# Gate and value products of two token blocks in seven half-size products a unit

## The chip, the cores and the metric

The kernel runs on one core of a Trainium2 chip. The metric is the device time of one execution in microseconds, the median over several executions.

## The reference, cut to what matters

Cosine-weighted linear attention over 8 batches of 8 heads, 576 positions and 64 features each, gives `x`, 4608 tokens of 512 features. Then a gated feed-forward block follows:

```python
g = x @ w_gate                                   # 512 -> 1536
gelu = 0.5 * g * (1.0 + erf(g * inv_sqrt2))
val = x @ w_val                                  # 512 -> 1536
return (gelu * val @ w_out).astype(np.float32)   # 1536 -> 512
```

## The kernel before

**Blocks and units.** The 4608 tokens are nine blocks of 512 (`NB` = 9, numbered 0 to 8). The work is written in an order by hand: the pools run under a manual schedule, so each engine executes its instructions in the order of the program. The token activations lie transposed in SBUF, `xT[n]`, 128 partitions by 4 feature chunks (`CT`) by 512 tokens. A gate-and-value unit (`gv_unit`, lines 392 to 412) makes one of the twelve slices (`JT` = 12) of 128 hidden features of a block: four matmuls over the chunks into one PSUM bank with `wg_sb`, four into the next with `wv_sb` (line 401, 512 columns each), a Gelu on ScalarE from PSUM to `gel` (409), and a product on VectorE of `gel` with the value bank, written as bfloat16 to `hT[n]` (410). Units take the bank pairs 0-1 and 2-3 in turn.

**Output products.** The output projection of block n-1 runs between the units of block n. It is already done with seven products in place of eight, per group `p` of 128 tokens in each half of the block (two groups a block). `h_sum` (484 to 494) makes the operand sums S1 to S4 of `hT` on VectorE, 128x768 in bfloat16; `wo_sum` made those of `w_out` once (T1 to T4). `product` (503 to 543) issues six matmuls of 256 columns (510) into the halves of bank 4 or into bank 5, copies products 1, 6 and 7 to SBUF on ScalarE (`u`, 530) while TensorE goes on accumulating in the same place, and adds on VectorE into `o_sb` (524). Finished tiles are stored from SP's queue (`flush`, 423).

**The loop.** The main loop (743 to 823) runs blocks 1 to 8 and, inside, the twelve units. After each unit come one or two products of the block before (772; two in units 0 and 6, one in the others, fourteen a block) and the sums that the table `SUMS` names (774). Until block 6 it also holds the attention work of the next batch: `kv_unit`, `nm_unit`, `prep`, transposes by DMA (`turn_q`, `turn_x`). In blocks 7 and 8 there is no attention work left; for block 8, `h_sum` makes its own S3 at units 8 and 9, and at unit 11 the first four of six slices of S1, S2 and S4 (752 to 757). The tail (826 to 838) does the fourteen products of block 8 with the last two slices of the sums ahead of them.

**Tiles that the change takes over.** The input tiles `qf`, `kf`, `vf` (two buffers each), the mapped inputs `qp` and `kp`, and `qT` are not used for attention any more in the last blocks.

Of the kernel before, what the change touches and what calls it, by code (L numbers as in the profile page):

```python
# [9 lines left out]
FP32 = mybir.dt.float32  # L10
BF16 = mybir.dt.bfloat16
AF = mybir.ActivationFunctionType
ALU = mybir.AluOpType
# [3 lines left out]
def kernel(  # L17
# [13 lines left out]
    nc = tc.nc  # L31
# [3 lines left out]
    C = H * D  # L35
# [29 lines left out]
    def bank(i):  # L65
        return ps[:, i]
# [356 lines left out]
    def flush(engs=(nc.sync, nc.sync)):  # L423
        for i, o_sb in stores:
            store(engs, i, o_sb)
        stores.clear()
# [45 lines left out]
    def place(n, p, name, cols, dtype):  # L472

        if n < NB - 1:
            return sums.tile([128, cols], dtype, name=name)
        was = "q" if name[0] == "u" else "kv"[p]
        if was not in rest:
            n_el = 8 * CH if was == "q" else 4 * JH * 128
            rest[was] = [inp.tile([128, n_el], dtype, name=was + "f"), 0]
        t, at = rest[was]  # L480
        rest[was][1] += cols
        return t[:, at:at + cols]

    def h_sum(n, p, name, j0=0, j1=JH):
        a = hs.setdefault((n, p), h_parts(n, p))
        if name not in a:
            a[name] = place(n, p, name, JH * 128, BF16).rearrange("q (j t) -> q j t", j=JH)
        x, y, op = {
            "S1": ("A21", "A22", ALU.add),
            "S2": ("S1", "A11", ALU.subtract),  # L490
            "S3": ("A11", "A21", ALU.subtract),
            "S4": ("A12", "S2", ALU.subtract),
        }[name]
        nc.vector.tensor_tensor(a[name][:, j0:j1], a[x][:, j0:j1], a[y][:, j0:j1], op=op)  # L494

    PROD = {
        1: ("A11", "B11"), 2: ("A12", "B21"), 3: ("S4", "B22"), 4: ("A22", "T4"),
# [5 lines left out]
    def product(n, p, i, u, m, v):  # L503


        a, b = PROD[i]
        key = n, p
        at = {1: u, 6: u, 7: u, 5: m, 3: m, 2: v, 4: v}[i]
        for j in range(JH):
            nc.tensor.matmul(  # L510
                at,
                lhsT=hs.setdefault(key, h_parts(n, p))[a][:, j],
                rhs=ts[b][:, j],
                start=(j == 0 and i in (1, 2, 4, 5)),
                stop=(j == JH - 1),
                skip_group_check=i in (3, 6, 7),
            )
        if key not in got:
            got[key] = [outp.tile([128, C], FP32, name="o_sb") for _ in range(2)]
        lo, hi = got[key]  # L520
        last = n == NB - 1

        def add(o, k, x, op=ALU.add):
            nc.vector.tensor_tensor(o, got[key, k], x, op=op)  # L524

        if i in (1, 6, 7) or last and i == 5:
            if last and i == 7:
                add(hi[:, RIGHT], 5, u)
            got[key, i] = place(n, p, f"u{i}", CH, FP32)
            nc.scalar.copy(got[key, i], at)  # L530
        if i == (2 if last else 1):
            add(lo[:, LEFT], 1, v)
        if i == 7 and not last:
            add(hi[:, RIGHT], 7, m)
        if i == 4:
            add(hi[:, LEFT], 7, v, ALU.subtract)
        if i == 3:
            add(lo[:, RIGHT], 6, m)
        if i in (3, 4):
            flush()  # L540
            stores.append((4 * n + 2 + p, hi) if i == 4 else (4 * n + p, lo))
            if last:
                flush((nc.sync, nc.scalar if p == 1 and i == 4 else nc.sync))


    HALF = BLK // 2
# [171 lines left out]
    for n in range(4, B - 2):  # L718
# [6 lines left out]
    SUMS = {  # L725
        2: {0: "1", 1: "2", 2: "34", 3: "56", 6: "78"},
        3: {0: "1", 1: "23", 2: "4", 3: "56", 4: "7", 6: "8"},
        8: {0: "1", 1: "2", 2: "3", 3: "4", 6: "5", 7: "6", 8: "7", 9: "8"},
    }
    for n in range(4, 8):  # L730
        SUMS[n] = {0: "1", 1: "23", 2: "4", 3: "5", 4: "6", 5: "7", 6: "8"}


    q3 = {
# [5 lines left out]
        (2, 1): ((8,), ()),  # L740
    }
    turn[0] = 1
    for n in range(1, NB):
        b = n + 1

        t_kv, t_nm, t_turn = {1: (7, 9, 12), 2: (6, 7, 11), 3: (2, 5, 9)}.get(n, (1, 2, 8))
        for jt in range(JT):
# [1 line left out]
                nm_unit(2, jt - t_nm, (6, 4, 6)[jt - t_nm])  # L749
                turn_x(2, jt - t_nm)  # L750
            heads = (0, 2, 4, 2)[n] if n < 4 else 0
            if n == NB - 1 and jt in (8, 9):
                h_sum(n, jt - 8, "S3")
            if n == NB - 1 and jt == JT - 1:
                for p in range(2):
                    for name in ("S1", "S2", "S4"):
                        h_sum(n, p, name, 0, JH - 2)
            if jt >= heads:
                gv_unit(n, jt)
            else:  # L760
# [60 lines left out]
                        turn_x(c, i)  # L821
            if n == 1 and 4 <= jt < 8:
                wo_sum(f"T{jt - 3}")


    for what in (
        ["S1", "S2", "S4", (0, 1), (1, 1), (0, 2, 0 + 2 * (turn[0] % 2)), (0, 5), (0, 6)]
        + ["T1", "T2", "T4", (1, 2, 1 + 2 * (turn[0] % 2)), (0, 3), (0, 7), (1, 5), (0, 4, 0)]
        + [(1, 6), (1, 3), (1, 7), (1, 4, 1)]
    ):  # L830
        if isinstance(what, str):
            h_sum(NB - 1, "ST".index(what[0]), "S" + what[1], JH - 2, JH)
        else:
            p, i = what[:2]
            to = (what[2:] or (0,))[0]
            product(
                NB - 1, p, i, ps[:, 4 + 2 * p, 0:CH], ps[:, 5 + 2 * p, 0:CH], ps[:, to, 0:CH]
            )


# [28 lines left out]
```

## Time and profile before

| | |
|---|---|
| median of 3 runs | 318.5 us (318.33 to 318.73) |
| the profiled execution | 319.06 us |
| its span, first to last instruction | 316.9 us |
| TensorE clock granted, mean | 0.996 |
| blocks 7 and 8, from the first matmul of block 7 to the last of the tail | 243.3 to 312.1 us |
| PE busy in 243.3 to 273.2 | 29.74 of 29.90 us |

A page or a view comes from one execution under the hardware profiler. PE is TensorE's matmul row, PEld its weight loads, which overlap it, DVE is VectorE, ACT ScalarE, POOL GpSimd, SP the queue that issues most DMAs. A matmul's recorded length includes its way through the pipeline, so matmuls in a row start closer together than their lengths say; their pace is read from start to start. Some matmul records are missing. "Idle before" is the time for which an engine had nothing that could start, with the instruction that released it. The chain is followed back from the last instruction, each step to what it waited for.

### The profile page before, as it was taken

To read this page: it belongs to the slowest core of one execution; us is meant where nothing else is said; L and a number is where in the kernel's file an instruction comes from. 1 tells how busy PE (TensorE), PEld (TensorE's weight loads), DVE (VectorE), ACT (ScalarE), POOL (GpSimd) and SP (SyncE) were. 2 spreads that over 40 slices of the span, in tenths; PEclk is the share of its full clock that TensorE was granted. 3 is DMA by queue.
4 is the path that set the end of the run, shared out by engine and by line. 5 is a ranking of instruction groups with operands and counts; after the bars stand their busy time and mean duration, and the time that the engine had idled before them with its cause. 6 is when DMAs were issued, how large, how long until landed. Compare 5 with 4: busy or idle time off the path is not lost.

```text
span 316.9 us, 7015 instructions
## 1 busy us (share of the span) xinstructions
PE 306.9 (97%) x2692; PEld 191.8 (61%) x2727; DVE 224.7 (71%) x542; ACT 159.4 (50%) x356; POOL 26.0 (8%) x43
## 2 busy tenths in 40 slices
PE   8899999999999999999999999999999999999994
PEld 2574455655866676666665566556666565656583
DVE  5854695699897996798687859695944554454782
ACT  7864675956474754466328632773232323232321
POOL 6674430000000000000000000000000000000000
PEclk9999999999999999999999999999999999999998
DMA  7999999871798946995993699175342020202025
GB/s 268 245 178 245 312 320 402 259 149 38 241 202 300 304 99 179 370 163 133 319 272 88 152 369 232 34 150 109 76 86 50 17 68 0 66 2 67 2 67 132
DMA packets 68945, 53.61 MB, mean 169 GB/s; under 512 B 45360, under 2 KB 54064, under 8 KB 68912
## 3 DMA queue, kind: packets, MB, share of 16 engines
q1 hardware_dynamic: 59184, 41.23, 49.7%
q0 software_dynamic: 9648, 11.80, 16.1%
q8 instruction: 21, 0.34, 0.4%
q10 hardware_dynamic: 80, 0.13, 0.1%
q14 instruction: 12, 0.10, 0.1%
HBM read 37.75 MB, written 9.44 MB: 149 GB/s over the span
## 4 chain that ended last, share of the span: by engine, by line
PE 86%; DMA 8%; issue 1%; DVE 1%; POOL 1%; SPq 0%; ACT 0%; DVEq 0%; POOLq 0%
PE ps L401 56%; PE ps L510 23%; DMA qf<-in_q_dram 4%; PE ps L283 3%; PE ps L242 2%; DMA vf<-in_v_dram 2%; DMA wv_sb<-in_moe_w_val_dram 2%; PE ps L373 1%; PE ps L431 1%; PE ps L358 0%; DVE x_sb L296 0%; SPq L81 0%; POOL wg_sb L95 0%; DVE o_sb L524 0%; POOL gate L560 0%
## 5 line engine op out<-in xcount | busy, mean ns | idle before, releaser
L410 DVE TENSOR_TENSOR hT<-gel,ps 128x512 bf16<-128x512 f32 (+1 forms) x114 | 73.5, 648 | 55.8 <-PE ps L401 50.3
L401 PE MATMUL ps<-xT,wv_sb 128*128 128x512 bf16 (+1 forms) x450 | 109.4, 364 | 0.3
L401 PE MATMUL ps<-xT,wg_sb 128*128 128x512 bf16 (+1 forms) x431 | 107.4, 363 | 1.5 <-issue 0.3
L409 ACT ACTIVATE gel<-ps 128x512 f32<-128x512 f32 (+1 forms) x114 | 64.4, 566 | 78.6 <-PE ps L401 72.3
L401 PEld LDWEIGHTS <-wv_sb 128*128 128x128 bf16 x456 | 44.6, 98 | 47.1
L401 PEld LDWEIGHTS <-wg_sb 128*128 128x128 bf16 x456 | 41.7, 98 | 28.2 <-issue 0.3
L510 PEld LDWEIGHTS <-S 128*128 128x128 bf16 x336 | 32.9, 98 | 14.9 <-DVE S L494 0.9
L530 ACT COPY u<-ps 128x256 f32<-128x256 f32 x42 | 15.6, 372 | 43.4 <-PE ps L510 43.4
L510 PE MATMUL ps<-T,S 128*128 128x256 bf16 x252 | 34.4, 273 | 0.0
L161 ACT ACTIVATE qp<-qf,sin_t 128x256 bf16<-128x256 f32 x72 | 32.0, 501 | 3.7 <-DMA qf<-in_q_dram 3.7
L524 DVE TENSOR_TENSOR o_sb<-u,ps 128x256 f32<-128x256 f32 x56 | 23.4, 418 | 14.4 <-ACT u L530 14.4
L510 PEld LDWEIGHTS <-hT 128*128 128x128 bf16 x288 | 28.2, 98 | 8.8
L161 ACT ACTIVATE kp<-kf,sin_t 128x256 bf16<-128x256 f32 (+1 forms) x73 | 30.0, 480 | 1.0 <-DMA kf<-in_k_dram 1.0
L296 DVE TENSOR_TENSOR x_sb<-ps,rec 128x512 bf16<-128x512 f32 x38 | 26.3, 692 | 2.0 <-DMA xT<-x_sb 0.5
L163 DVE TENSOR_SCALAR qp<-qf,cos_t 128x256 bf16<-128x256 f32 x71 | 22.0, 357 | 3.3 <-DMA qf<-in_q_dram 3.3
L510 PE MATMUL ps<-wo_sb,hT 128*128 128x256 bf16 x192 | 23.6, 273 | 0.0
L163 DVE TENSOR_SCALAR kp<-kf,cos_t 128x256 bf16<-128x256 f32 x63 | 18.2, 349 | 0.0
L283 PEld LDWEIGHTS <-qT 128*128 128x128 bf16 x304 | 14.6, 98 | 2.8 <-ACT qT L588 0.3
L283 PE MATMUL ps<-kv_sb,qT 128*128 128x65 bf16 x304 | 16.0, 194 | 0.0
L494 DVE TENSOR_TENSOR S<-hT 128x768 bf16<-128x768 bf16 x28 | 15.4, 552 | 0.0
L510 PE MATMUL ps<-T,hT 128*128 128x256 bf16 x96 | 13.1, 273 | 0.2
L180 DVE CAST vx<-vf 128x1152 bf16<-128x1152 f32 (+1 forms) x15 | 11.9, 802 | 1.0 <-DMA vf<-in_v_dram 1.0
(84 smaller groups left out, 204.8 us busy)
## 6 DMA issues: line engine op xcount, KB each, us to landing
out_dram<-o_sb SPq DMA_DIRECT2D x71, 128.0 KB, 2.5
kf<-in_k_dram SPq DMA_DIRECT2D x12, 576.0 KB, 7.2
vf<-in_v_dram SPq DMA_DIRECT2D x12, 576.0 KB, 8.7
qf<-in_q_dram SPq DMA_DIRECT2D x10, 576.0 KB, 5.2
qf<-in_q_dram POOLq DMA_DIRECT2D x4, 576.0 KB, 12.4
kf<-in_k_dram POOLq DMA_DIRECT2D x4, 576.0 KB, 12.5
vf<-in_v_dram POOLq DMA_DIRECT2D x4, 576.0 KB, 12.6
wg_sb<-in_moe_w_gate_dram POOLq DMA_DIRECT2D x6, 256.0 KB, 6.8
```

The source lines that it names most:

```text
L161: nc.scalar.activation(o, i, AF.Relu, scale=tab[:, j:j + 1])
L163: (eng or nc.vector).tensor_scalar(o, i, 0.0, tab[:, j:j + 1], op0=ALU.max, op1=ALU.mult)
L180: copy(vx_tiles[b % 2][:, m0:m1, j0:j1, 0:D], staged["v", b][:, m0:m1, j0 * D:j1 * D].rearrange("p m (j d) -> p m j d", d=D),)
L283: nc.tensor.matmul(bank(b0 + h // 4)[:, (h % 4) * (D + 1):(h % 4 + 1) * (D + 1)], lhsT=q_cols(b, t, h), rhs=kv_sb[b][:, h // 2, h % 2, :], ...
L296: nc.vector.tensor_tensor(x, nm[:, :, :, 0:D], rec[:, :, :, None].to_broadcast([128, 2, 4, D]), op=ALU.mult,)
L401: nc.tensor.matmul(bank(b0 + g)[:, 0:w], lhsT=wt[:, ct, js], rhs=xt[:, ct, c0:c0 + w], start=(ct == 0), stop=(ct == CT - 1),)
L409: nc.scalar.activation(gel[:, 0:w], bank(b0)[:, 0:w], AF.Gelu)
L410: nc.vector.tensor_mul(hT[n][:, jt, c0:c0 + w], gel[:, 0:w], bank(b0 + 1)[:, 0:w])
L494: nc.vector.tensor_tensor(a[name][:, j0:j1], a[x][:, j0:j1], a[y][:, j0:j1], op=op)
L510: nc.tensor.matmul(at, lhsT=hs.setdefault(key, h_parts(n, p))[a][:, j], rhs=ts[b][:, j], start=(j == 0 and i in (1, 2, 4, 5)), stop=(j == ...
L524: nc.vector.tensor_tensor(o, got[key, k], x, op=op)
L530: nc.scalar.copy(got[key, i], at)
```

## The change

**Units of blocks 7 and 8.** The loop runs blocks 1 to 6 (`FAST` = 7). For blocks 7 and 8 a new `fast_unit` treats gate and value weights together as a 2 by 2 matrix of blocks: rows are gate and value, columns the lower and upper two of the four feature chunks; the right-hand side is `xT[n]`, split by the same chunks and by halves of 256 tokens. Seven products replace eight. Each is two matmuls of 256 columns. The partial results are combined in place: product 1 goes to one of the banks 2, 6, 7, is copied by ScalarE into half of bank 0, where product 2 is added on top; product 6 is added onto 1, copied to SBUF (`U6`), then product 7 and later 4 are added in the same place. Product 5 goes to bank 3 or 1, is copied to SBUF (`M5`), and product 3 is added onto it. VectorE adds `U6` and that bank into SBUF (`G2`, the gate of the second half of the tokens), and `M5` and product 7 back into the bank in PSUM (the value of the second half). Two Gelus and two products of 256 columns replace one of each of 512.

**Two units at a time.** In step t, products 1 and 5 of unit t come first, then product 7 of unit t-1, the output products (`o_step`) of one unit, products 6, 2 and 3 of unit t, and product 4 of unit t-1. So 25 steps serve 24 units, and `o_step` lags by one step.

**Sums.** `w_sum` makes S1 to S4 of the two weights (128x2x1536, in three pieces each, twelve instructions of 128x2x512) on VectorE in block 6, at units 0, 1 and 7 to 11. `x_sum` makes T1 to T4 of a block's `xT` (128x512): those of block 7 at units 8 to 11 of block 6, those of block 8 after steps 2, 4, 6 and 8 of block 7. The operand sums `h_sum` of blocks 6 and 7, and most of those of block 8, move from VectorE to GpSimd; block 8's second group keeps three on VectorE, in the tail, whole.

**Tail.** One product of block 8 moves into the last step; the thirteen others have a new order, with product 3 of the second group last. Product 5's contribution comes from its SBUF copy, so one VectorE addition there has two SBUF inputs. The stores of both last tiles use SP's and ScalarE's queue.

In the instruction order of TensorE, 144 matmuls and 144 weight loads come on top: 24 units by 14 - 8.

```diff
--- before.py
+++ after.py
@@ -473,15 +473,15 @@
 
         if n < NB - 1:
             return sums.tile([128, cols], dtype, name=name)
-        was = "q" if name[0] == "u" else "kv"[p]
+        was = "kp" if name[0] == "u" else ("kf", "vf")[p]
         if was not in rest:
-            n_el = 8 * CH if was == "q" else 4 * JH * 128
-            rest[was] = [inp.tile([128, n_el], dtype, name=was + "f"), 0]
+            pool, n_el = (attn, 8 * CH) if was == "kp" else (inp, 4 * JH * 128)
+            rest[was] = [pool.tile([128, n_el], dtype, name=was), 0]
         t, at = rest[was]
         rest[was][1] += cols
         return t[:, at:at + cols]
 
-    def h_sum(n, p, name, j0=0, j1=JH):
+    def h_sum(n, p, name, j0=0, j1=JH, eng=nc.vector):
         a = hs.setdefault((n, p), h_parts(n, p))
         if name not in a:
             a[name] = place(n, p, name, JH * 128, BF16).rearrange("q (j t) -> q j t", j=JH)
@@ -491,7 +491,7 @@
             "S3": ("A11", "A21", ALU.subtract),
             "S4": ("A12", "S2", ALU.subtract),
         }[name]
-        nc.vector.tensor_tensor(a[name][:, j0:j1], a[x][:, j0:j1], a[y][:, j0:j1], op=op)
+        eng.tensor_tensor(a[name][:, j0:j1], a[x][:, j0:j1], a[y][:, j0:j1], op=op)
 
     PROD = {
         1: ("A11", "B11"), 2: ("A12", "B21"), 3: ("S4", "B22"), 4: ("A22", "T4"),
@@ -524,14 +524,12 @@
             nc.vector.tensor_tensor(o, got[key, k], x, op=op)
 
         if i in (1, 6, 7) or last and i == 5:
-            if last and i == 7:
-                add(hi[:, RIGHT], 5, u)
             got[key, i] = place(n, p, f"u{i}", CH, FP32)
             nc.scalar.copy(got[key, i], at)
         if i == (2 if last else 1):
             add(lo[:, LEFT], 1, v)
-        if i == 7 and not last:
-            add(hi[:, RIGHT], 7, m)
+        if i == 7:
+            add(hi[:, RIGHT], 7, got[key, 5] if last else m)
         if i == 4:
             add(hi[:, LEFT], 7, v, ALU.subtract)
         if i == 3:
@@ -540,7 +538,119 @@
             flush()
             stores.append((4 * n + 2 + p, hi) if i == 4 else (4 * n + p, lo))
             if last:
-                flush((nc.sync, nc.scalar if p == 1 and i == 4 else nc.sync))
+                flush((nc.sync, nc.scalar if p == 1 else nc.sync))
+
+    FAST = NB - 2
+    CP = CT // 2
+    wa, xb, temps = {}, {}, {}
+
+    def w_sum(name, j0, j1):
+        if not wa:
+            wa["A11"], wa["A12"] = wg_sb[:, 0:CP], wg_sb[:, CP:CT]
+            wa["A21"], wa["A22"] = wv_sb[:, 0:CP], wv_sb[:, CP:CT]
+        if name not in wa:
+            was = {"S1": "qf", "S2": "qf", "S3": "kf", "S4": "vf"}[name]
+            wa[name] = inp.tile([128, CP, J], BF16, name=was)
+        x, y, op = {
+            "S1": ("A21", "A22", ALU.add),
+            "S2": ("S1", "A11", ALU.subtract),
+            "S3": ("A11", "A21", ALU.subtract),
+            "S4": ("A12", "S2", ALU.subtract),
+        }[name]
+        nc.vector.tensor_tensor(
+            wa[name][:, :, j0:j1], wa[x][:, :, j0:j1], wa[y][:, :, j0:j1], op=op
+        )
+
+    def x_sum(n, i):
+        if n not in xb:
+            xt = xT[n]
+            xb[n] = {
+                "B11": xt[:, 0:CP, 0:256], "B12": xt[:, 0:CP, 256:512],
+                "B21": xt[:, CP:CT, 0:256], "B22": xt[:, CP:CT, 256:512],
+            }
+        if "x" not in temps:
+            temps["x"] = attn.tile([128, 2, 4, CP, 256], BF16, name="qp")
+        b = xb[n]
+        x, y = (("B12", "B11"), ("B22", "T1"), ("B22", "B12"), ("B21", "T2"))[i]
+        b[f"T{i + 1}"] = temps["x"][:, n - FAST, i]
+        nc.vector.tensor_tensor(b[f"T{i + 1}"], b[x], b[y], op=ALU.subtract)
+
+    GV = {
+        1: ("A11", "B11"), 2: ("A12", "B21"), 3: ("S4", "B22"), 4: ("A22", "T4"),
+        5: ("S1", "T1"), 6: ("S2", "T2"), 7: ("S3", "T3"),
+    }
+    gels = {}
+
+    def fast_unit(t, between):
+
+        def at(i, t):
+            if i == 2:
+                return ps[:, 0, 256 * (t % 2):256 * (t % 2) + 256]
+            return bank((3, 1)[t % 2] if i in (3, 5) else (2, 6, 7)[t % 3])[:, 0:256]
+
+        def mm(i, t):
+            n, jt = FAST + t // JT, t % JT
+            a, b = GV[i]
+            for ct in range(CP):
+                nc.tensor.matmul(
+                    at(i, t),
+                    lhsT=wa[a][:, ct, jt * 128:(jt + 1) * 128],
+                    rhs=xb[n][b][:, ct],
+                    start=(ct == 0 and i in (1, 5)),
+                    stop=(ct == CP - 1),
+                    skip_group_check=i not in (1, 5),
+                )
+
+        def tmp(i, t):
+            if "t" not in temps:
+                temps["t"] = attn.tile([128, 6, 256], FP32, name="qT")
+            return temps["t"][:, 2 * i + t % 2]
+
+        def h(t, half):
+            n, jt = FAST + t // JT, t % JT
+            if n not in hT:
+                hT[n] = ffn.tile([128, JT, BLK], BF16, name="hT")
+            return hT[n][:, jt, 256 * half:256 * half + 256]
+
+        def gelu(t, half, src):
+            if t not in gels:
+                gels[t] = ffn.tile([128, BLK], FP32, name="gel")
+            nc.scalar.activation(gels[t][:, 256 * half:256 * half + 256], src, AF.Gelu)
+
+        new, old = t < 2 * JT, t > 0
+        M5, U6, G2 = range(3)
+        if new:
+            mm(1, t)
+            nc.scalar.copy(at(2, t), at(1, t))
+            mm(5, t)
+            nc.scalar.copy(tmp(M5, t), at(5, t))
+        if old:
+            mm(7, t - 1)
+            gelu(t - 1, 1, tmp(G2, t - 1))
+            nc.vector.tensor_tensor(at(3, t - 1), tmp(M5, t - 1), at(7, t - 1), op=ALU.add)
+            nc.vector.tensor_tensor(
+                h(t - 1, 1), gels[t - 1][:, 256:512], at(3, t - 1), op=ALU.mult
+            )
+        between()
+        if new:
+            mm(6, t)
+            nc.scalar.copy(tmp(U6, t), at(6, t))
+            mm(2, t)
+            gelu(t, 0, at(2, t))
+            mm(3, t)
+            nc.vector.tensor_tensor(tmp(G2, t), tmp(U6, t), at(3, t), op=ALU.add)
+        if old:
+            mm(4, t - 1)
+            nc.vector.tensor_tensor(
+                h(t - 1, 0), gels[t - 1][:, 0:256], at(4, t - 1), op=ALU.mult
+            )
 
     HALF = BLK // 2
@@ -725,10 +835,12 @@
     SUMS = {
         2: {0: "1", 1: "2", 2: "34", 3: "56", 6: "78"},
         3: {0: "1", 1: "23", 2: "4", 3: "56", 4: "7", 6: "8"},
-        8: {0: "1", 1: "2", 2: "3", 3: "4", 6: "5", 7: "6", 8: "7", 9: "8"},
+        8: {i: str(i + 1) for i in range(8)},
     }
     for n in range(4, 8):
         SUMS[n] = {0: "1", 1: "23", 2: "4", 3: "5", 4: "6", 5: "7", 6: "8"}
+
+    W_SUMS = {0: (0,), 1: (1,), 7: (2, 3, 4), 8: (5, 6), 9: (7, 8), 10: (9, 10), 11: (11,)}
 
     q3 = {
@@ -740,7 +852,7 @@
         (2, 1): ((8,), ()),
     }
     turn[0] = 1
-    for n in range(1, NB):
+    for n in range(1, FAST):
         b = n + 1
 
         t_kv, t_nm, t_turn = {1: (7, 9, 12), 2: (6, 7, 11), 3: (2, 5, 9)}.get(n, (1, 2, 8))
@@ -749,12 +861,6 @@
                 nm_unit(2, jt - t_nm, (6, 4, 6)[jt - t_nm])
                 turn_x(2, jt - t_nm)
             heads = (0, 2, 4, 2)[n] if n < 4 else 0
-            if n == NB - 1 and jt in (8, 9):
-                h_sum(n, jt - 8, "S3")
-            if n == NB - 1 and jt == JT - 1:
-                for p in range(2):
-                    for name in ("S1", "S2", "S4"):
-                        h_sum(n, p, name, 0, JH - 2)
             if jt >= heads:
                 gv_unit(n, jt)
             else:
@@ -821,21 +927,54 @@
                         turn_x(c, i)
             if n == 1 and 4 <= jt < 8:
                 wo_sum(f"T{jt - 3}")
+            if n == FAST - 1:
+                for i in W_SUMS.get(jt, ()):
+                    w_sum(f"S{i // 3 + 1}", 512 * (i % 3), 512 * (i % 3) + 512)
+                if jt >= 8:
+                    x_sum(FAST, jt - 8)
+
+    def o_step(n, jt):
+        p, u = divmod(jt, 6)
+        for i in ((2, 1), (5,), (6,), (7,), (4,), (3,))[u]:
+            product(n - 1, p, i, ps[:, 4, 0:CH], ps[:, 5, 0:CH], ps[:, 4, CH:C])
+        for i in map(int, SUMS[n].get(jt, "")):
+            h_sum(n - 1, i // 5, f"S{(i - 1) % 4 + 1}", eng=nc.gpsimd)
+        if jt % 3 == 1:
+            flush()
+
+    for t in range(2 * JT):
+        n, jt = FAST + t // JT, t % JT
+        if n == NB - 1 and jt in (9, 10):
+            h_sum(n, jt - 9, "S3", eng=nc.gpsimd)
+        fast_unit(t, lambda: o_step(FAST + (t - 1) // JT, (t - 1) % JT) if t else None)
+        if (n, jt) == (NB - 1, JT - 2):
+            for name in ("S1", "S2", "S4"):
+                h_sum(n, 0, name, 0, JH - 2, eng=nc.gpsimd)
+        if n == FAST and jt in (2, 4, 6, 8):
+            x_sum(NB - 1, jt // 2 - 1)
+
+    def last_product(p, i, to=0):
+        product(
+            NB - 1, p, i, ps[:, (4, 6)[p], 0:CH], ps[:, (5, 7)[p], 0:CH], ps[:, to, 0:CH]
+        )
+
+    def ends():
+        o_step(NB - 1, JT - 1)
+        last_product(0, 1)
+
+    fast_unit(2 * JT, ends)
 
     for what in (
-        ["S1", "S2", "S4", (0, 1), (1, 1), (0, 2, 0 + 2 * (turn[0] % 2)), (0, 5), (0, 6)]
-        + ["T1", "T2", "T4", (1, 2, 1 + 2 * (turn[0] % 2)), (0, 3), (0, 7), (1, 5), (0, 4, 0)]
-        + [(1, 6), (1, 3), (1, 7), (1, 4, 1)]
+        [(1, 1), "S1", "S2", "S4", (0, 2, 0), (0, 5), (0, 6), "T1", "T2", "T4"]
+        + [(1, 2, 1), (0, 3), (0, 7), (1, 5), (1, 6), (0, 4, 0), (1, 7), (1, 4, 1), (1, 3)]
     ):
         if isinstance(what, str):
-            h_sum(NB - 1, "ST".index(what[0]), "S" + what[1], JH - 2, JH)
+            p = "ST".index(what[0])
+            h_sum(NB - 1, p, "S" + what[1], (JH - 2, 0)[p], JH)
         else:
-            p, i = what[:2]
-            to = (what[2:] or (0,))[0]
-            product(
-                NB - 1, p, i, ps[:, 4 + 2 * p, 0:CH], ps[:, 5 + 2 * p, 0:CH], ps[:, to, 0:CH]
-            )
+            last_product(*what)
 
 # ---- launch: one core; inputs and outputs as the reference has them ----
```

## The prediction

> **What bounds the kernel now.** I read the page's engine table, the chain of waits, the busy time by stretch, the groups by shape, and the timeline around block 8's start, in this order.
>
> ```profile
> PE 306.9 (97%) x2692; PEld 191.8 (61%) x2727; DVE 224.7 (71%) x542; ACT 159.4 (50%) x356; POOL 26.0 (8%) x43
> ```
>
> TensorE looks full, but a recorded matmul includes its way through the pipeline, so its pace must come from the chain (start, length, work):
>
> ```profile
> 298.34 1.73 PE ps L401 x8
> 300.07 0.66 PE ps L510 x6
> 300.72 1.73 PE ps L401 x8
> 302.45 9.18 PE ps L510 x84
> ```
>
> Eight 512-column matmuls take 1.727 us (0.2159 each); 84 of 256 columns take 9.18 (0.1093 each; six 0.656). Nothing lies between: blocks 7 and 8 with the tail should need 24 x 1.727 + 42 x 0.656 = 69.0 us at that pace, and run from 243.3 to 312.1, 68.8. They hold no stall worth naming, so only fewer columns can shorten them. By stretch (PE, PEld, DVE, ACT busy):
>
> ```profile
> 243.30:273.20 29.90, 29.74 (x179) 17.61 (x180) 15.02 (x29) 9.40 (x18) 0.00 (x0) 1.00 0.16 36
> 273.20:302.40 29.20, 29.04 (x174) 17.02 (x175) 16.56 (x34) 9.40 (x18) 0.00 (x0) 1.00 0.14 33
> ```
>
> Here VectorE is half idle, ScalarE two thirds, GpSimd wholly. Lengths by shape:
>
> ```profile
> L410 DVE TENSOR_TENSOR hT<-gel,ps 128x256 bf16<-128x256 f32 x16 | 6.3, 418 | 1.4 <-ACT gel L409 1.3
> L409 ACT ACTIVATE gel<-ps 128x256 f32<-128x256 f32 x16 | 6.2, 392 | 4.5 <-PE ps L401 3.8 <-DVE rec L295 0.6
> L530 ACT COPY u<-ps 128x256 f32<-128x256 f32 x42 | 15.6, 372 | 43.4 <-PE ps L510 43.4
> L494 DVE TENSOR_TENSOR S<-hT 128x768 bf16<-128x768 bf16 x28 | 15.4, 552 | 0.0
> L163 POOL TENSOR_SCALAR kp<-kf,sin_t 128x128 bf16<-128x128 f32 x2 | 3.3, 1642 | 2.2 <-DMA kf<-in_k_dram 2.2
> ```
>
> Handovers, from the timeline:
>
> ```profile
> 273.05 1.03 PE L401 MATMUL ps<-xT,wg_sb 128*128 128x512 bf16 x4
> 273.92 1.03 PE L401 MATMUL ps<-xT,wv_sb 128*128 128x512 bf16 x4
> 274.12 0.60 ACT L409 ACTIVATE gel<-ps 128x512 f32<-128x512 f32 x1 [1.78 <-PE ps L401]
> 274.78 1.47 PE L510 MATMUL ps<-wo_sb,hT 128*128 128x256 bf16 x12
> 275.05 0.69 DVE L410 TENSOR_TENSOR hT<-gel,ps 128x512 bf16<-128x512 f32 x1 [1.36 <-PE ps L401]
> ```
>
> When TensorE moves on from the gate matmuls (273.92), ScalarE starts 0.20 later; from the value matmuls (274.78) VectorE 0.27 later. Consecutive VectorE instructions that need not wait start about 0.085 earlier than their lengths say (in block 6 a 0.55 sum is followed after 0.47).
>
> [...]
>
> **The change part by part, against the profiled execution (319.06 us; span 316.9, 2.16 around it).**
>
> *TensorE work.* A unit goes from 8 x 0.2159 = 1.727 to 14 x 0.1093 = 1.530 us. 24 units save 24 x 0.197 = 4.7 us, all on the path, if TensorE stays dense. TensorE's instruction order has the 144 extra matmuls that this needs.
>
> *Does it stay dense?* I lay out a step with one output product; times from its start. TensorE: product 1 to 0.22, 5 to 0.44, 7 of the older unit to 0.66, output product to 1.31, 6 to 1.53, 2 to 1.75, 3 to 1.97, 4 of the older unit to 2.19.
> ScalarE: copy of 1 from 0.42 to 0.79 (0.372; the PSUM-to-PSUM form is not in the trace: 0.28, a copy's start to the next one's when nothing waits, to 0.50, line 161's row; I take the copy's); copy of 5 to 1.1; Gelu of the older unit's second half from SBUF ([...]at most the 501 of line 161) to 1.6; in three steps of six a `u` copy to 1.9; copy of 6, ready at 1.73, to 2.1 or 2.25; Gelu of the first half to 2.5 or 2.65. The next step's first copy can start at 2.19 + 0.42 = 2.61. That fits, with 0.1 spare at worst.
> VectorE: addition of `M5` and 7 into PSUM, 0.93 to 1.35 (PSUM output unseen: 0.33, the row less the overlap, to 0.69, the 512-column row; I take 0.418); product after the Gelu, 1.63 to 2.05; an `o_sb` addition in four steps of six, to 2.4; `G2` to 2.8; product with 4, to 3.15, which is 0.96 of the next step, where the next addition is just ready.
> TensorE's new waits have room: product 6 (copy of 1; queued behind it 2, 3, 4) needs 0.79 and starts at 1.31; 3 needs 1.1, starts 1.75; the next step's 7 needs 2.25, starts 2.63; 4 (waits for the `M5` addition; behind it is the next step) needs 1.4, starts 1.97. Each margin is 0.4 to 0.6 us, so the unseen forms at their upper ends (0.13 and 0.27 longer) still fit. Steps with two products have 0.66 more. I charge 0.2 us for all 24.
>
> *Filling the pipeline.* Step 0 has no output product between 5 and 6: 6 would start at 0.44, but waits for the copy of 1 until 0.22 + 0.20 + 0.37 + 0.08 = 0.87. +0.4 us, uncovered. The last step drains under two products (1.3 us), free.
>
> *Weight sums and block 7's `x_sum` in block 6.* Sums of 256, 512 and 768 columns take 284, 418 and 552 ns, so 1024 take 0.69, or 0.60 apart: twelve are 7.2 us, four `x_sum` 1.4. Units 7 to 10 then ask VectorE for 2.1 to 2.6 us in a period of 2.38 (1.727 + 0.656): a lag of about 0.6. A unit's banks are needed again after the next unit and two output products, 1.5 us after the product that frees them, and the first fast step uses the bank pair freed longer. Cost 0, at most 0.5.
>
> *Sums on GpSimd.* [...]each is made one to two steps ahead. The only GpSimd arithmetic row, 1642 ns for 128 columns, bounds from above: if it is all per column, 9.9 us each; if fixed, 3.3. Lower end 0.55, VectorE's own. I take 1.7: free, since each sum lies beside the units and output products of the steps ahead of its use; from 3.4 on that cover is gone (rival B). VectorE loses 16 x 0.55, off the path.
>
> *Four `x_sum` in block 7.* [...] Behind it in VectorE's queue stands the `M5` addition, behind that TensorE's product 4. With sums back to back to about 13 us after block 7's start, the `x_sum` after steps 2 and 4 (7.2, 11.5) meet one, that after 6 perhaps. Wait 0 to 1.7 less the margin of 0.5: 0 to 1.2 each; I take 0.7 in all, range 0 to 2.5.
>
> *Tail.* The same 42 products. VectorE's three whole sums of the second group (1.5 us) come after the first group's three parts; by this table S1 is ready some 2 us ahead of the product that uses it. Before, the last addition waited behind the copy of product 7 and the store went out at 312.97, 0.85 after the last matmul; now product 3 is last: 0.27 + 0.42 + 0.03 = 0.72. -0.1. Storing by ScalarE adds one DMA issue there (0.56) behind its last copy; SP has one fewer. Stores in the loop go out a step later on an SP queue that has only them.
>
> Sum: -4.7 + 0.2 + 0.4 + 0.7 - 0.1 = -3.5. Profiled: 319.06 - 3.5 = 315.6; it lies 0.56 above the median of the runs, so 315.0 as a median.
>
> **The rivals.**
> *A. Two-engine steps bind (partly a gain).* If handovers between ScalarE and VectorE cost more than here, a step takes ScalarE's length, not TensorE's. For it: ScalarE has 2.0 of 2.19 us asked in a plain step and 2.3 with a copy, without overlap. Against: margins above. A mean step before is 1.727 + 14/12 x 0.656 = 2.49, dense 2.30; at 2.40 the saving is 24 x 0.09 = 2.2, less 0.4, 0.7, plus 0.1: 317.3.
> *B. GpSimd is the bound (slower).* Place: the `S` operands of output products. It decides from 27.6 / 8 = 3.4 us a sum, where eight no longer fit in a block; for it speaks the 1642 ns row. At 4.0 each block stretches to 32 us: 2 x 4.4 more against 3.5 saved gives 323.8. Against: that row ran in the kernel's opening, beside VectorE instructions with two SBUF inputs.
> *C. GpSimd's sums also block VectorE instructions with one SBUF input (slower).* 16 sums x (1.7 - 0.5) = 19 us at most; it turns slower from 0.22 us a sum. Half of it: 324.5.[...]
>
> **How the numbers follow.** Forecast 64% (its own ends: 0.7 less for `x_sum`, 0.2 for steps, 1.8 and 0.5 more for `x_sum` and block 6), A 15%, B 7%, C 8%, and 6% for a mix of A and longer `x_sum` waits that eats the gain. A measurement of this kernel can tell about 0.2%, 0.6 us, from no change. Faster: 64 and 12 of A, 76%; within: 3 of A and 3 of the mix, 6%; slower: 3 of the mix, B and C, 18%. The range takes in A and the mix up to no change and leaves B and C out: 313.6 (a dense run with a few tenths besides) to 318.7.
>
> **What would show it.** Right: in blocks 7 and 8 matmuls 0.109 apart without gaps, steps of 2.19 and 2.84 us, the last matmul near 308.7 (312.1 - 4.7 + 1.3). GpSimd sums near 1.7 us; `x_sum` in block 7 longer or late. Wrong: idle TensorE before products 6, 3 or 4 in each step (A), before weight loads of `S` (B), or VectorE products and additions starting at the ends of GpSimd sums (C).

## The result and the profile after

The changed kernel takes 315.95 us (315.65 to 316.82, four runs) against 318.44 (318.33 to 318.73, four runs) before: a ratio of 0.9925, 95% interval 0.9904 to 0.9946. It is 2.5 us faster; the forecast was 3.5, with a time of 315.0. The profiled spans are 314.3 and 316.9 us.

Below, "the stretch" is the time from the start of block 7's first matmul to the start of the tail's last, plus 0.11 us for the pace of that one, in one profiled execution. Before, block 7's first matmul starts at 243.16, not at 243.3 as the table of before has it:

```profile
243.16 1.03 PE L401 MATMUL ps<-xT,wg_sb 128*128 128x512 bf16 x4
```

So the stretch is 68.95 us before (243.16 to 312.11) and 66.49 after (242.74 to 309.23). What lies ahead of it varies by over a microsecond between kernels that are the same up to there (block 7 starts at 242.38 in e1_held below, at 244.15 in e2_vector), so the stretch tells small differences better than the totals do. Two pairs of executions with the same TensorE order and no stall agree in it to 0.01 us: before and e4_sums_alone (68.95), e9_late and e10_stores (64.85).

The engine line of the page after:

```profile
PE 301.8 (96%) x2842; PEld 205.6 (65%) x2871; DVE 248.2 (79%) x610; ACT 183.0 (58%) x452; POOL 59.1 (19%) x64
```

TensorE is recorded busy for 5.1 us less, VectorE and ScalarE for 23.5 and 23.6 more. Whether TensorE stays dense, two views tell. First the busy time by stretch (length, then PE, PEld, DVE, ACT, POOL with their instructions, then the granted clock, the DMA share and GB/s), then the chain of waits (start, length, work):

```profile
242.70:268.90 26.20, 24.40 (x221) 21.39 (x220) 23.53 (x53) 18.63 (x59) 13.50 (x8) 1.00 0.18 41
268.90:298.00 29.10, 29.10 (x269) 26.08 (x268) 23.40 (x61) 22.50 (x72) 17.53 (x12) 1.00 0.16 38
```

```profile
256.33 0.66 PE ps L510 x6
256.98 1.53 PE ps L602 x14
258.51 0.66 PE ps L510 x6
259.17 1.53 PE ps L602 x14
260.70 1.31 PE ps L510 x12
262.01 1.53 PE ps L602 x14
...
300.87 8.53 PE ps L510 x78
```

In the second stretch TensorE is busy for the whole 29.10 us, and the chain has fourteen matmuls in 1.53 us and six in 0.66, with nothing between: steps of 2.19 and 2.84 us, as laid out. The idle time is all in the first stretch: 1.80 us. The groups by shape give the lengths of what the kernel before did not have:

```profile
L494 POOL TENSOR_TENSOR S<-hT 128x768 bf16<-128x768 bf16 x8 | 13.3, 1662 | 211.7 <-DVE hT L410 198.6 <-PE ps L602 12.5 <-PE ps L510 0.6
...
L625 ACT ACTIVATE gel<-qT 128x256 f32<-128x256 f32 x24 | 10.3, 429 | 2.8 <-DVE qT L648 2.8
...
L637 DVE TENSOR_TENSOR ps<-qT,ps 128x256 f32<-128x256 f32 x24 | 10.2, 426 | 0.8
...
L631 ACT COPY ps<-ps 128x256 f32<-128x256 f32 x24 | 8.6, 357 | 6.3 <-PE ps L602 6.2
...
L566 DVE TENSOR_TENSOR vf<-wg_sb,qf 128x1024 bf16<-128x1024 bf16 x3 | 3.3, 1130 | 0.0
...
L582 DVE TENSOR_TENSOR qp<-xT,qp 128x512 bf16<-128x512 bf16 x4 | 3.2, 812 | 0.0
...
L582 DVE TENSOR_TENSOR qp<-xT 128x512 bf16<-128x512 bf16 x3 | 1.9, 637 | 0.0
```

The last three rows stand out: weight sums (L566) and `x_sum` (L582) have means of 1130, 812 and 637 ns, while the same shapes take 682 and 418 elsewhere. The timeline at the start of block 7 shows where (start, length, engine, line; in brackets the idle time before and what ended it):

```profile
242.92 0.68 DVE L410 TENSOR_TENSOR hT<-gel,ps 128x512 bf16<-128x512 f32 x1
...
243.52 0.41 DVE L524 TENSOR_TENSOR o_sb<-u,ps 128x256 f32<-128x256 f32 x1
243.62 0.38 PE L602 MATMUL ps<-qp,qf 128*128 128x256 bf16 x2 [0.28 <-ACT ps L631]
...
243.69 1.64 POOL L494 TENSOR_TENSOR S<-hT 128x768 bf16<-128x768 bf16 x1 [198.62 <-DVE hT L410]
...
243.85 2.03 DVE L566 TENSOR_TENSOR vf<-wg_sb,qf 128x1024 bf16<-128x1024 bf16 x1
...
245.41 1.97 POOL L494 TENSOR_TENSOR S<-S,hT 128x768 bf16<-128x768 bf16 x1
245.80 1.85 DVE L582 TENSOR_TENSOR qp<-xT,qp 128x512 bf16<-128x512 bf16 x1
...
248.09 0.43 DVE L637 TENSOR_TENSOR ps<-qT,ps 128x256 f32<-128x256 f32 x1
...
248.57 0.38 PE L602 MATMUL ps<-qp,wv_sb 128*128 128x256 bf16 x2 [1.52 <-DVE ps L637]
```

GpSimd's first sum starts at 243.69. The last weight sum, left over from block 6, starts 0.16 later and lasts 2.03 us instead of 0.68: it ends 0.55 after GpSimd's sum. The same happens with T4 and GpSimd's second sum (1.85 instead of 0.42). The view books no wait here; the wait is inside the instruction's own length. Behind them in VectorE's order stands the addition into PSUM (L637), behind that product 4. The two are late by 1.35 + 1.43 = 2.78 us, and TensorE loses 1.68 from the pace, that is, from the starts of the matmuls (1.52 of it is booked as a wait).

### The profile page after: what moved, and what is told of

Its sections match the earlier page's. It is cut to its first block, busy times and chain, and to the rows that moved or that the text cites. A ratio compares the mean times of both kernels' runs of the same rounds, so it can differ in the third digit from the quotient of the medians.

```text
span 314.3 us, 7602 instructions
## 1 busy us (share of the span) xinstructions
PE 301.8 (96%) x2842; PEld 205.6 (65%) x2871; DVE 248.2 (79%) x610; ACT 183.0 (58%) x452; POOL 59.1 (19%) x64
## 4 chain that ended last, share of the span: by engine, by line
PE 83%; DMA 7%; DVE 5%; issue 2%; SPq 1%; POOL 0%; ACT 0%; DVEq 0%; POOLq 0%
PE ps L401 42%; PE ps L510 23%; PE ps L602 11%; DMA qf<-in_q_dram 4%; PE ps L283 3%; DMA vf<-in_v_dram 3%; PE ps L242 2%; DVE qp L582 1%; PE ps L373 1%; DVE qp L163 1%; DVE hT L410 1%; SPq L81 1%; PE ps L431 1%; DVE o_sb L524 0%; PE ps L358 0%
## 5 line engine op out<-in xcount | busy, mean ns | idle before, releaser
L401 PE MATMUL ps<-xT,wv_sb 128*128 128x512 bf16 (+1 forms) x354 | 84.7, 360 | 0.2
L401 PE MATMUL ps<-xT,wg_sb 128*128 128x512 bf16 (+1 forms) x341 | 83.4, 359 | 1.2 <-issue 0.3
L409 ACT ACTIVATE gel<-ps 128x512 f32<-128x512 f32 (+1 forms) x90 | 50.1, 558 | 50.8 <-PE ps L401 45.0
L410 DVE TENSOR_TENSOR hT<-gel,ps 128x512 bf16<-128x512 f32 (+1 forms) x90 | 56.8, 636 | 26.8 <-PE ps L401 21.3
L401 PEld LDWEIGHTS <-wv_sb 128*128 128x128 bf16 x360 | 35.2, 98 | 35.8
L494 POOL TENSOR_TENSOR S<-hT 128x768 bf16<-128x768 bf16 x8 | 13.3, 1662 | 211.7 <-DVE hT L410 198.6
L401 PEld LDWEIGHTS <-wg_sb 128*128 128x128 bf16 x360 | 32.3, 98 | 21.9 <-issue 0.2
L602 PE MATMUL ps<-qp,qf 128*128 128x256 bf16 x96 | 18.3, 272 | 0.3 <-ACT ps L631 0.3
L602 PE MATMUL ps<-xT,wg_sb 128*128 128x256 bf16 x96 | 18.3, 273 | 0.0
```

Source lines behind the costliest of these rows:

```text
L401: nc.tensor.matmul(bank(b0 + g)[:, 0:w], lhsT=wt[:, ct, js], rhs=xt[:, ct, c0:c0 + w], start=(ct == 0), stop=(ct == CT - 1),)
L409: nc.scalar.activation(gel[:, 0:w], bank(b0)[:, 0:w], AF.Gelu)
L410: nc.vector.tensor_mul(hT[n][:, jt, c0:c0 + w], gel[:, 0:w], bank(b0 + 1)[:, 0:w])
L494: eng.tensor_tensor(a[name][:, j0:j1], a[x][:, j0:j1], a[y][:, j0:j1], op=op)
L602: nc.tensor.matmul(at(i, t), lhsT=wa[a][:, ct, jt * 128:(jt + 1) * 128], rhs=xb[n][b][:, ct], start=(ct == 0 and i in (1, 5)), stop=(ct == ...
```

## The experiments

**Theory:** the missing microsecond is this collision. **Rivals:** the two-unit pipeline itself is slow to fill, or VectorE is overloaded by work left from block 6, with GpSimd or without it. Each edit is of the changed kernel except where said; e7, e8 and e11 do one operation twice with the same result.

**e1_held.** GpSimd's first sum is held until T4 is there.

```diff
+        if (n, jt) == (FAST, 0):
+            nc.gpsimd.tensor_copy(gate2, xb[FAST]["T4"][:, 0, 0:1])
         for i in map(int, SUMS[n].get(jt, "")):
             h_sum(n - 1, i // 5, f"S{(i - 1) % 4 + 1}", eng=nc.gpsimd)
```

> The changed kernel, with GpSimd's first sum held until VectorE has made T4 of block 7 (one small copy on GpSimd that reads T4). Nothing else differs. Theory (GpSimd's first two sums hold the last weight sum, 2.03 us instead of 0.68, and T4, 1.85 instead of 0.42[...], and product 4 of unit 0 waits 1.68 us for what stands behind them): both come back to their usual length, the wait goes, and the stretch from block 7's first matmul to the last of the tail falls from 66.5 to about 64.9 us; in all about 1.6 us less, 314.3. Rival (VectorE simply comes late out of block 6 and the pipeline has to fill): the wait stays at over 1 us, time within 0.4 us of the changed kernel.

Measured: 314.42 us, ratio to before 0.9872 (0.9843 to 0.9900); stretch 65.02, 1.47 less than after. Its timeline:

```profile
243.26 0.38 PE L602 MATMUL ps<-qp,qf 128*128 128x256 bf16 x2 [0.28 <-ACT ps L631]
...
243.50 0.68 DVE L566 TENSOR_TENSOR vf<-wg_sb,qf 128x1024 bf16<-128x1024 bf16 x1
...
244.10 0.41 DVE L582 TENSOR_TENSOR qp<-xT,qp 128x512 bf16<-128x512 bf16 x1
...
244.66 0.18 POOL L942 CAST gate<-qp 128x1 f32<-128x1 bf16 x1 [200.62 <-DVE qp L582]
...
246.53 0.38 PE L602 MATMUL ps<-qp,wv_sb 128*128 128x256 bf16 x2
```

VectorE does the same instructions in the same order, at 0.68 and 0.41 us, and product 4 (246.53) has no wait any more. VectorE's load alone was not the cause; GpSimd beside it was. The fill's 0.28 stays. What is missing of the 1.68 went to one of block 8's `x_sum`, which took 1.14 us here: TensorE loses 0.39 behind it, from the pace.

**e3_early.** The weight sums and block 7's `x_sum` are made earlier in block 6.

```diff
-    W_SUMS = {0: (0,), 1: (1,), 7: (2, 3, 4), 8: (5, 6), 9: (7, 8), 10: (9, 10), 11: (11,)}
+    W_SUMS = {0: (0, 1), 1: (2, 3), 7: (4, 5), 8: (6, 7), 9: (8, 9), 10: (10, 11)}
...
-                if jt >= 8:
-                    x_sum(FAST, jt - 8)
+                if 7 <= jt < 11:
+                    x_sum(FAST, jt - 7)
```

> The changed kernel, with the weight sums and block 7's operand sums one unit earlier in block 6, so that none is left for VectorE after unit 10. Theory (collision with GpSimd's first sums): as with the held GpSimd, 1.6 us less, stretch about 64.9, 314.3; VectorE in block 6 carries the same work, and no unit of block 6 gets slower. Rival (lag out of block 6): if the weight sums themselves are too much for VectorE there, moving them forward stalls TensorE in units 7 to 10 of block 6, and the gain is under half of it.

Measured: 314.63 us, 0.9871 (0.9844 to 0.9898); stretch 65.13. The collision is avoided from the other side, by VectorE's work being done before GpSimd starts, and the gain is that of e1. One of block 8's `x_sum` took 1.25 us here and cost TensorE 0.50 from the pace (0.24 is booked as a wait).

**e2_vector.** All operand sums back on VectorE.

```diff
-            h_sum(n - 1, i // 5, f"S{(i - 1) % 4 + 1}", eng=nc.gpsimd)
+            h_sum(n - 1, i // 5, f"S{(i - 1) % 4 + 1}", eng=nc.vector)
```

(and the same in the two other calls.)

> The changed kernel, with all operand sums of hT back on VectorE; GpSimd does no arithmetic beside it. Theory: a step asks VectorE for 4 x 0.335 + 0.22 + 0.31 = 1.9 us, start to start, of 2.30, so TensorE stays dense but for a few tenths where sums stand ahead of the addition that product 4 waits for; without GpSimd there is no collision, so the wait of 1.68 us goes: stretch 64.9 to 66, about 314.5 to 315.3, faster than the changed kernel. Rival (GpSimd's sums are what makes the change pay): VectorE falls behind, with product 4 waiting in most steps: 24 x 0.1 to 0.2 us, 318 or more.

Measured: 316.59 us, 0.9941 (0.9922 to 0.9960); stretch 66.52, as after (the intervals of the ratios overlap). No instruction is stretched (all `x_sum` 416 to 419 ns), but VectorE runs late: the chain goes through its sums and products in the first steps of block 7, and the last step waits 0.67 for L637. So as the change was made, what GpSimd's help brought was eaten by the collision. With the collision gone (e1) it is worth 66.52 - 65.02 = 1.5 us.

**e4_sums_alone.** The kernel before, with the operand sums of blocks 6 and 7 on GpSimd, by an argument `eng` of `h_sum`.

```diff
                     h_sum(
                         n - 1, i // 5, f"S{(i - 1) % 4 + 1}",
+                        eng=nc.gpsimd if n >= NB - 2 else nc.vector,
                     )
```

> The kernel before, with the operand sums of blocks 6 and 7 on GpSimd and nothing else changed. Theory: VectorE is half idle there and TensorE dense, so nothing moves but the first products that use a sum, which may wait a few tenths for the slower sum (1.66 against 0.55 us): 318.4 to 319. Rival (relief of VectorE is part of the gain): faster by over 0.5 us.

Measured: 317.91 us, 0.9988 (0.9970 to 1.0005); stretch 68.95, as before. Sixteen sums of 1.64 us on GpSimd change nothing by themselves: in this run TensorE is busy for all of the 58.26 us from 242.24 on, VectorE for 23.32, GpSimd for 25.98.

**e5_filled.** The last output product of block 5, which ran at the end of block 6, moves between products 5 and 6 of step 0, to fill the pipeline.

```diff
+                    if (n, jt) != (FAST - 1, JT - 1):
...
-o_step(FAST + (t - 1) // JT, (t - 1) % JT) if t else None)
+o_step(FAST + (t - 1) // JT, (t - 1) % JT) if t else left())
```

(`left` makes `product(FAST - 2, 1, 3, ...)`.)

> The changed kernel, with the last output product of block 5 (six matmuls, 0.66 us) moved from the end of block 6 into step 0, between its products 5 and 6. Theory: the 0.45 us for which product 6 of unit 0 waits for the copy of product 1 are covered. But product 4 of unit 0 waits for VectorE's late operand sum, which this doesn't move, so that wait grows by about as much: within 0.2 us of the changed kernel, stretch in all the same (block 7's first matmul 0.66 earlier, last one at the same time). Rival (the two waits add up independently): 0.45 us less.

Measured: 315.37 us, 0.9898 (0.9879 to 0.9918); stretch 66.47 less 0.656 for the moved product, 65.81: 0.68 gained, more than either the theory (0.2 at most) or the rival (0.45) had. The move also changed who came first. Its timeline:

```profile
243.39 0.68 DVE L566 TENSOR_TENSOR vf<-wg_sb,qf 128x1024 bf16<-128x1024 bf16 x1
...
243.56 2.35 POOL L494 TENSOR_TENSOR S<-hT 128x768 bf16<-128x768 bf16 x1 [199.27 <-DVE hT L410]
...
243.99 0.41 DVE L582 TENSOR_TENSOR qp<-xT,qp 128x512 bf16<-128x512 bf16 x1
...
249.18 1.65 POOL L494 TENSOR_TENSOR S<-hT,S 128x768 bf16<-128x768 bf16 x1
...
249.44 1.67 DVE L582 TENSOR_TENSOR qp<-xT 128x512 bf16<-128x512 bf16 x1
...
251.50 0.38 PE L602 MATMUL ps<-qp,wv_sb 128*128 128x256 bf16 x2 [0.65 <-DVE ps L637]
```

The moved product's `o_sb` addition no longer stands ahead of the weight sum on VectorE. So the weight sum starts 0.17 ahead of GpSimd's sum and keeps its 0.68; GpSimd's takes 2.35 instead of 1.64. As in after, the one that starts second is stretched; but T4, right behind the weight sum, starts 0.43 after GpSimd's sum and still keeps its 0.41. Both waits at the start are gone, 2.1 us from the pace. But two `x_sum` for block 8 now meet a sum (1.67 and 1.48 us), and TensorE loses some 1.6 us behind them (the first wait is booked with 0.65), against 0.1 in after.

**e6_both.** The edits of e3 and e5 together.

> The changed kernel, with the sums of block 6 one unit earlier and block 5's last output product in step 0. Theory: both waits go, 1.7 + 0.45 us: TensorE dense from block 7 to the end, 588 matmuls x 0.1093 = 64.3 us after block 7's first matmul, with the moved product 64.9; about 313.8. Rival (the waits come back elsewhere, in block 6 or in later steps): less than 1.6 us gained on the changed kernel.

Measured: 314.49 us, 0.9875 (0.9855 to 0.9895); stretch 65.78, less 0.656: 65.12, no better than e3. The fill is gone; an `x_sum` of block 8 gives it back:

```profile
253.49 1.65 POOL L494 TENSOR_TENSOR S<-hT 128x768 bf16<-128x768 bf16 x1
...
253.93 1.49 DVE L582 TENSOR_TENSOR qp<-xT,qp 128x512 bf16<-128x512 bf16 x1
...
255.81 0.38 PE L602 MATMUL ps<-qp,wv_sb 128*128 128x256 bf16 x2 [0.48 <-DVE ps L637]
```

**e9_late.** e6, with block 8's `x_sum` after steps 8 to 11, where the first run of GpSimd's sums is over.

```diff
-        if n == FAST and jt in (2, 4, 6, 8):
-            x_sum(NB - 1, jt // 2 - 1)
+        if n == FAST and jt >= 8:
+            x_sum(NB - 1, jt - 8)
```

> The version with earlier sums in block 6 and the filled step 0, and besides block 8's four operand sums (x_sum) after steps 8 to 11 of block 7 in place of 2, 4, 6 and 8, where GpSimd has made its last sum of block 6 and has none of block 7 to make yet. Theory (what is left of stalls there, 0.8 us, is x_sum waiting for GpSimd's sums, with product 4 behind it): no x_sum is longer than 0.45 us, TensorE is dense from block 7's first matmul, 64.9 us with the moved product (588 + 6 matmuls x 0.1093), 0.8 us less than without the change, about 313.7. Rival (the rest lies in the steps themselves): x_sum gets shorter, but the stretch stays within 0.3 us of 65.8.

Measured: 313.33 us, 0.9829 (0.9810 to 0.9848): faster than both kernels, 5.3 us below before. The busy time by stretch, of after and of this run, over the stretch of each:

```profile
242.74:309.23 66.49, 64.69 (x590) 57.40 (x587) 55.03 (x134) 45.40 (x140) 33.14 (x21) 1.00 0.20 45
```

```profile
241.90:306.75 64.85, 64.85 (x595) 58.02 (x593) 51.34 (x133) 45.42 (x140) 32.60 (x21) 1.00 0.20 47
```

TensorE is busy for 64.85 of 64.85 us, with one product more in it than after has. VectorE has 3.7 us less busy time, nearly all of it waiting that had been recorded as work (2.78 at block 7's start, 0.8 in block 8's `x_sum`). No `x_sum` is over 418 ns.

**e7_act_more and e8_dve_more.** Which of the two engines is close to its limit: ScalarE's copy of product 6 twice (e7), or VectorE's addition that makes `G2` twice (e8).

```diff
             nc.scalar.copy(tmp(U6, t), at(6, t))
+            nc.scalar.copy(tmp(U6, t), at(6, t))
```

```diff
             nc.vector.tensor_tensor(tmp(G2, t), tmp(U6, t), at(3, t), op=ALU.add)
+            nc.vector.tensor_tensor(tmp(G2, t), tmp(U6, t), at(3, t), op=ALU.add)
```

> The changed kernel, with the copy of product 6 on ScalarE issued twice in each step (the same values to the same place). It measures the margin on ScalarE. Theory (what counts is the pace from start to start, about 0.28 us a copy): a step then asks 1.77 us, 2.05 with an output copy, of 2.19: no change within 0.5 us. Rival (the lengths add up, 2.36 us a plain step and 2.73 with a copy): ScalarE becomes the bound, 24 x 0.2 us or more, 321 or more.

> The changed kernel, with the addition that makes G2 on VectorE issued twice in each step. It measures the margin on VectorE. Theory (0.335 us from start to start): a step asks 5 x 0.335 + 0.22 = 1.9 of 2.30 us, and the 0.5 us of margin ahead of product 4 takes it: within 0.7 us of the changed kernel. Rival (lengths and handovers add up, 2.5 us a step): 24 x 0.2 us, 320 or more.

Measured: e7 316.33 us, 0.9931 (0.9906 to 0.9956), stretch 67.01, 0.52 more than after, most of it (0.37) in the last step. e8 318.79, 1.0009 (0.9993 to 1.0025), stretch 68.76, 2.27 more. ScalarE takes 24 more copies for half a microsecond. VectorE's 24 additions cost the whole gain, far more than expected. Since e8 still had the collisions, it was repeated without them.

**e11_late_dve.** e9 with the edit of e8.

> The version with all three moves, with the addition that makes G2 on VectorE issued twice in each step. In the changed kernel the same doubling cost 2.3 us of the stretch. Theory (VectorE's own margin is as worked out, and most of those 2.3 us were longer waits at the collisions with GpSimd): without the collisions at most 0.7 us more than without the doubling. Rival (the chain of handovers through VectorE sets the steps from there on): still 1.5 us more or over, spread over many steps.

Measured: 315.74 us, 0.9918 (0.9893 to 0.9943); stretch 67.32, 2.47 more than e9. So the collisions are not why it costs so much. Busy time in a part of the stretch, and the timeline:

```profile
256.30:272.50 16.20, 15.77 (x138) 13.26 (x137) 14.83 (x42) 11.83 (x37) 1.72 (x2) 1.00 0.22 51
```

```profile
268.36 0.42 DVE L582 TENSOR_TENSOR qp<-xT 128x512 bf16<-128x512 bf16 x1
...
268.69 0.42 DVE L637 TENSOR_TENSOR ps<-qT,ps 128x256 f32<-128x256 f32 x1
...
269.16 0.38 PE L602 MATMUL ps<-qp,wv_sb 128*128 128x256 bf16 x2 [0.21 <-DVE ps L637]
...
273.78 0.94 PE L510 MATMUL ps<-wo_sb,hT 128*128 128x256 bf16 x7 [0.31 <-DVE hT L652]
...
300.09 0.38 PE L602 MATMUL ps<-qp,wv_sb 128*128 128x256 bf16 x2 [0.41 <-DVE ps L637]
```

From the pace, TensorE loses 1.35 us in and right behind the four steps with an `x_sum`, 0.47 at an output product that waits for the last of block 7's `hT` (273.78), and 0.57 in the last step, which has no products of a newer unit (300.09). No other step loses more than 0.04, so the loss is not spread over many steps as the rival had it. A step with an `o_sb` addition and an `x_sum` now has seven VectorE instructions. Back to back they start about 0.335 apart (0.418 less 0.085; here 268.36 to 268.69), so the step asks 7 x 0.335 = 2.35 us and TensorE gives 2.19. A step with six asks 2.01 and loses nothing. In e9 the fullest steps have six: VectorE has under 0.2 us to spare in them. The other two places, 1.04 us together, lie where little TensorE work covers the chain from VectorE to TensorE; that reading is argued from the order and not tried.

**e10_stores.** e9 with ScalarE's queue used for the last store only.

```diff
-nc.scalar if p == 1 else nc.sync))
+nc.scalar if p == 1 and i == 3 else nc.sync))
```

> The version with all three moves (sums of block 6 earlier, step 0 filled, block 8's operand sums later), with ScalarE's queue used for one of the last four stores of the second group, as before the change, and SP's for three. It tests why the changed kernel ends 5.1 us after its last matmul where the kernel before ends 4.8 after. Theory (two stores of 0.6 to 0.7 us in a row on ScalarE's queue hold the last one by 0.1 us, which SP's queue with three in a row would hold longer): 0.1 to 0.6 us later than with two on ScalarE. Rival (ScalarE's second issue is what costs): 0.1 to 0.3 us earlier.

Measured: 314.10 us, 0.9862 (0.9840 to 0.9884); same stretch, 64.85, and the span ends 5.29 us after the last matmul instead of 5.04. SP's five issues now end at 308.48, later than both queues in e9 (308.20). By the traces, two stores on ScalarE's queue are better by 0.25 us; the intervals of the two ratios just overlap.

## Why the prediction was right, and which term was off

| step | predicted, us | measured in the stretch, us |
|---|---|---|
| fourteen half-size matmuls for eight | -4.7 | 68.95 to 588 x 0.1093 = 64.27: -4.7 |
| steps not dense, block 8's `x_sum` | +0.2, +0.7 | +0.1 together |
| filling the pipeline | +0.4 | +0.45 |
| weight sums and block 7's `x_sum` in block 6 | 0, at most 0.5 | +1.68 |
| tail | -0.1 | +0.24 |

The measured terms come to -2.2; the stretch with the tail shows -2.46 + 0.24 = -2.2, the spans -2.6 and the medians -2.5. The remaining 0.4 us of the spans lies ahead of block 7 (first matmul at 242.74 instead of 243.16), where single executions differ by more than that. That the total came within a microsecond is in part luck: a term that was put at nothing cost 1.68 us, and of 0.9 us charged for uneven steps and block 8's `x_sum` about 0.1 was paid.

**TensorE work, and whether it stays dense: right.** The prediction reads 68.8 us before; from 243.16 it is 68.95, still nearer to its sum of 69.0. From 256 us on it has no gap, on the layout's step lengths. The unseen forms were close to the values taken: the PSUM-to-PSUM copy 357 ns (taken 372), the addition into PSUM 426 (418), the Gelu from SBUF 429 (at most 501). The Gelu of the same shape from PSUM takes 396 in after, 33 ns less.

**Fill: right.** Product 6 of unit 0 starts at 243.62 instead of 243.17, released by the copy of product 1 (L631).

**The step that failed: "Weight sums and block 7's `x_sum` in block 6 ... Cost 0, at most 0.5".** It counted VectorE's lag of 0.6 us against the release of banks, and that was no cost. It did not follow VectorE's order on to where GpSimd's first two sums begin. The last weight sum and T4, both with two SBUF inputs, stand behind block 6's last `hT` product (L410, 242.92), and the same product releases GpSimd's first sum. An `o_sb` addition (243.52) lies between on VectorE, so GpSimd starts first. A lag moves both engines alike; the place in the order decides, as e5 shows, where that addition is gone and VectorE comes first. The prediction did have an `x_sum` wait for a GpSimd sum, which no trace of before showed, but charged it to block 8's alone. The margin was sized rightly: VectorE was 2.78 us late, TensorE lost 1.68, so 1.10 was covered, in a step with two output products (0.4 to 0.6 plus 0.66). e1 shows the cause by holding GpSimd, e3 by moving VectorE's work, e5 by a change of who comes first; e2, without GpSimd's sums, has no stretched instruction.

**Block 8's `x_sum`: 0.7 taken, about 0.1 paid.** This was luck of the timing: three of them took 857, 640 and 560 ns in after. With the block's start in another phase, single ones took 1.14 us in e1, 1.25 in e3, 1.67 in e5 and 1.49 in e6, and TensorE lost 0.4, 0.5, 1.6 and 0.9 us in all from the pace. So 0.7 was a fair mean, and the range of 0 to 2.5 holds all of them.

**Rival B (GpSimd the bound): refuted.** A sum takes 1.64 us undisturbed (e4); the prediction took 1.7, which no trace of before showed. **Rival C (instructions with one SBUF input blocked too): refuted.** With GpSimd busy for 33 us of the stretch, no addition or product of 256 columns with one SBUF and one PSUM operand took over 430 ns. **Rival A (two-engine steps bind): not in this kernel, but near**, and by VectorE rather than ScalarE: one more copy a step on ScalarE costs 0.52 us in all (e7), one more addition on VectorE 2.27 (e8) and 2.47 (e11).

**Tail: wrong sign, cause open.** Up to the last store's issue it is right: that issue starts 0.73 us after the last matmul, 0.86 before. ScalarE's queue, before and after:

```profile
312.97 0.56 ACTq L421 DMA_DIRECT2D out_dram<-o_sb  x1
```

```profile
309.30 1.38 ACTq L421 DMA_DIRECT2D out_dram<-o_sb  x2
```

But the second of two issues on ScalarE's queue takes 0.74 us, where the single one took 0.56, and its store lands 2.97 us after the issue starts instead of 2.63. The span ends some 1.3 us after that landing in both. In e10 the single store on ScalarE's queue took 3.05 us to land and SP's last one, which ended that kernel, 2.73, so two in a row on one queue are not the whole reason. What slows the landings was not tried by itself.

## What to carry to other kernels

When an operation moves to GpSimd, list every VectorE instruction with two SBUF inputs that can still be in its queue when GpSimd starts, work left over from the stage before included, and follow what stands behind it in VectorE's order up to TensorE (here a sum of 0.68 us took 2.03, and TensorE lost 1.68). An instruction whose mean is well above others of its shape may have a wait inside its length (here 1130 ns beside 682); look at its single records. Then put the two apart in time: here that, with the pipeline filled, was worth as much again as the change itself (2.5 us, then 2.6 from 315.95 to 313.33, medians of separate sets of runs; 2.3 in the stretch, with the moved product counted).

## What the hardware showed that was not expected

- Two-SBUF-input VectorE sums that started during a GpSimd sum ended 0.55 us (1024 columns, in after) or about 0.27 us (512; 0.27 in after, 0.28 in e6) after GpSimd's, less than their own 0.68 and 0.42. Before, sums of 256, 512 and 768 columns take 284, 418 and 551 ns, from which about 0.52 ns a column and 0.15 us fixed are worked out; so what follows GpSimd's end is about the columns' part alone (0.53 and 0.27). The one that started second was stretched in both orders: VectorE's from 0.68 to 2.03 us in after, GpSimd's from 1.64 to 2.35 in e5. T4 in e5 was not: directly behind the weight sum on VectorE, it started 0.43 us after GpSimd's sum and took 0.41, and GpSimd's sum ended 1.51 after it. In after, in the like place, GpSimd's second sum (245.41) went before T4; why is open.
- A GpSimd sum of 768 columns takes 1.64 us alone (e4), one of 512 columns 1.157 (after): from these two about 1.9 ns a column and 0.19 us fixed.
- Moving 0.656 us of TensorE work from one side of a block's border to the other took one VectorE addition out of the way and so changed which engine came first, by a third of a microsecond, and with it the sign of a wait. In this kernel a margin of 0.16 us did not survive a small edit.
